# A two-layer decode kernel: heads in twos, one on even and one on odd partitions, loaded in runs of 24576 B

## The chip, the core and the metric

The kernel runs on one core of a Trainium2 chip (trn2). The metric is device time in microseconds (us) of one launch; lower is better. Each kernel is run several times and the median counts. One execution is profiled: its trace tells, for each engine, when each instruction ran, and for the 16 DMA engines when each packet moved.

Names used below: PE is TensorE (matmuls; PEld its weight loads), DVE is VectorE, ACT is ScalarE, POOL is GpSimd, SP is the engine whose queue issues all DMAs here. L12 is line 12 of the kernel.

## What is computed

One token (B = S = 1, D = 640) goes twice through attention against a cache and then a small mixer with an MLP; both layers use the same weights and the same caches. Of 32768 cached positions the last W = 4096 are used, by 32 heads of width 192. All inputs are bf16.

```python
def attention(x, k_cache, v_cache, wq, wo):          # x: LayerNorm of the token
    q = (x @ wq) as 32 heads of 192
    k, v = k_cache[:, :, Sk - 4096:], v_cache[:, :, Sk - 4096:]
    p = softmax(q . k * 192 ** -0.5)                 # per head, over 4096 positions
    return concat over heads (p . v) @ wo
def mixer_mlp(x, w1, w2, w3, w4):
    ...
    return x1 + gelu(layernorm(x1) @ w3) @ w4
for _ in range(2):
    x = x + attention(layernorm(x), k_cache, v_cache, wq, wo)
    x = x + mixer_mlp(layernorm(x), w1, w2, w3, w4)
```

With S = 1 the shifted `w1`, `w2` branch of the mixer brings zeros, so `x1` is the mixer's input and only `w3` and `w4` are loaded. K and V of a layer are 32 heads x 2 x 1.57 MB, 100 MB; the work is small beside these bytes.

## The kernel before

**Cells.** SBUF holds 11 cells, each 128 partitions x 12288 B, as much as K or V of one head. `take` gives the cell that has been free longest, `give` puts it back. A cell holds K, V, a block of Wo (four heads), W3, W4, a transposed K that is kept for the second layer (`("T", h)`), or the area in which transposed quarters of K lie (`("area", layer)`, one cell, its four quarters in turn).

**The stream.** `layer_stream` writes out the order of all transfers of a layer by hand; `need(...)` issues them on SP in that order, as far as the one asked for. Per group of four heads it is K of the next group's head, V of this group's head, four times, and then Wo of the group. SP works in order: a transfer whose cell is not free yet holds up all that are behind it. Eight semaphores for DMAs are used in turn, so the ninth transfer also waits for the first one to land. Wq is loaded first; W3 and W4 close each layer.

**One head of K (L360 to L380, L443 to L456).** K of a head is loaded with 32 positions on each of the 128 partitions: one run of 12288 B a partition. `T` turns it on DVE in 32x32 blocks, a quarter at a time (L377, four a head). `scores`, called as `S`, multiplies it on PE with a block-diagonal Q (`Qblk`, 16 columns for the group's four heads by four parts; L453, 24 matmuls of 128x256 a head) and all four heads of a group add up in one half of the PSUM tile `ST_ps`.

**Softmax of a group (L473 to L540).** `part_max` and `full_max` reduce on DVE (L478, L488), PE turns and spreads the maxima (L483, L501), ACT forms Exp (L507), DVE turns P (L512), PE swaps it into place (L523) and ACT writes `PT` (L526).

**P.V (L560 to L576).** 16 matmuls a head (L569) with two columns of `PT` each write `O_ps`; DVE transposes `O_ps` for each head (L576), and `o_fold` brings the head's part into `oT` with small matmuls (L583, L588). The cell of V is given back behind the 16 matmuls.

**The order around it.** For each group: scores of the next group's first head while the softmax of this group runs; then for each head of this group its P.V, and T and S of the next group's next head.

**From layer to layer.** Groups go from heads 28 to 31 down to heads 0 to 3 in the first layer and upward in the second. Transposed K of heads 0 to 6 stays in cells (`NKEEP` = 7), V of head 3 (`VC`) too, V of head 2 (`VP`) is kept in PSUM and in the cell of Wo's block 0, a part of V of head 4 (`VX`) in `kx`. So the second layer starts with scores of heads 0 to 3 from kept cells, and with loads of V of heads 0 and 1, K of head 7, then K of head 8, V of head 4, and so on. In the first group of the second layer the P.V go in the order 3, 0, 1, 2. Cells that the loads there use: V of head 0 the cell of W3 (free after L901), V of head 1 the cell of W4 (free after L948), K of heads 7 and 8 the cells of T0 and T2 (free after the scores of heads 0 and 2, L453), V of heads 4 and 5 those of T3 and T6.

Of the kernel before, what the change touches and what calls it, by code (L numbers as in the profile page):

```python
# [35 lines left out]
def kernel(  # L36
# [33 lines left out]
    scale = float(Dh) ** -0.5  # L70
    eps = 1e-5
# [39 lines left out]

    loaded = {}
    free = deque(range(NCELL))
    cell_of = {}

    def take(key):
        i = free.popleft()
        cell_of[key] = i
        return cells.tile([P, FREE], BF16, tag=f"cell{i}", name=f"cell{i}")
# [9 lines left out]

    def load_k(layer, h):  # L130
        t = take(("k", layer, h))
        nc.sync.dma_start(t[:], A_k_cache[0, h, s0:Sk, :].rearrange("(p j) d -> p (j d)", p=P))
        return t

    def load_v(layer, h):
        t = take(("v", layer, h))
        src = A_v_cache[0, h, s0:Sk, :].rearrange("(p j) d -> p (j d)", p=P)
# [4 lines left out]
        for e in cut + (FREE,):  # L142
            kept_v = h == VP or h == VX and i > 0
            if layer == 0 or not kept_v:
                nc.sync.dma_start(v_pair(t, h, i, e - i), src[:, i:e])
            i = e
# [58 lines left out]
    def layer_stream(layer):  # L205
# [38 lines left out]
        return seq  # L244
# [4 lines left out]
    def need(*key):  # L249
        while key not in loaded:  # L250
            k = stream[pos[0]]
            pos[0] += 1
            loaded[k] = LOADERS[k[0]](*k[1:])
        return loaded[key]
# [9 lines left out]
    ones = const.tile([P, P], F32, name="ones")  # L264
    nc.vector.memset(ones[:], 1.0)
    Lf = wx_sb[:, 0:2 * P].bitcast(F32).rearrange("p (j i) -> p j i", j=4)
    nc.gpsimd.memset(Lf, 0.0)
    for base in (0, -1, -64, -65):
# [29 lines left out]
    nc.vector.tensor_reduce(out=hm[:], in_=ident[:].rearrange("p (q x m) -> p x q m", q=4, m=NM)[:, 0:QH],  # L298
                            op=ALU.add, axis=AX.XY)

    QW = QH * NM
    QHEAD = NCOL * QW
    QSLOT = QH * (QHEAD + NM)
# [18 lines left out]
    def ln_center(x, rowsum):  # L322

        mean_ps = psm.tile([P, 1], F32, tag="psm")
        nc.tensor.matmul(mean_ps[:], lhsT=ones[:], rhs=rowsum[:, 0:1], start=True, stop=True)
# [10 lines left out]
        def total():  # L336
            var_ps = psm.tile([P, 1], F32, tag="psm")
            nc.tensor.matmul(var_ps[:], lhsT=ones[:], rhs=ssq[:, 0:1], start=True, stop=True)
# [43 lines left out]
    def qproj_steps(c, xc, part=None, row=None):  # L382
# [49 lines left out]
        def block():  # L432
            nh = n * P // Dh
            h0 = 4 * (t0 - c * QT) // NCOL
            diag = Qblk[:, c % 2].rearrange("p (h r) -> p h r", h=QH)[:, h0:h0 + nh, 0:QHEAD]
            nc.vector.tensor_tensor(
                out=diag.rearrange("p h (f x) -> p h f x", x=QW)[:, :, :, 0:NM],
                in0=held["r"][:, :].rearrange("p (h f) -> p h f", h=nh).unsqueeze(3).broadcast_to([P, nh, NCOL, NM]),
                in1=blkm[:, :].unsqueeze(1).unsqueeze(1).broadcast_to([P, nh, NCOL, NM]), op=ALU.mult)
# [3 lines left out]
    def scores(h, Ts, q0, ST_ps, hq):  # L443

        ng = NGK // NT
        Q = Qblk[:, h // QH % 2, hq * QHEAD:(hq + 1) * QHEAD].rearrange("p (f x) -> p f x", x=QW)
# [26 lines left out]
    def softmax_steps(n, ST_ps, sc):  # L473
        held = {}

        def part_max():
            pm = big.tile([P, 1], F32, name="pm")
            nc.vector.tensor_reduce(out=pm[:], in_=ST_ps, op=ALU.max, axis=AX.X)  # L478
            held["pm"] = pm

        def turn_max():
            pmT_ps = psm.tile([1, P], F32, tag="psm")
            nc.tensor.transpose(pmT_ps[0:1, :], held["pm"][:, 0:1], ident[:, :])  # L483
            held["pmT"] = pmT_ps

        def full_max():
            ngm = big.tile([1, 2 * QH], F32, name="ngm")
            nc.vector.tensor_reduce(out=ngm[:], in_=held["pmT"][0:1, :].rearrange("o (q x m) -> o x q m", q=4, m=NM),  # L488
                                    op=ALU.max, axis=AX.XY, negate=True)
            held["PrT"] = o_bytes[:, SW:2 * SW]  # L490

            wide = held["PrT"][0:1, :].bitcast(F32)
            nc.vector.tensor_scalar(
                out=wide.rearrange("o (q x m) -> o q x m", q=4, m=NM),
                in0=ngm[:].unsqueeze(1).unsqueeze(3).broadcast_to([1, 4, 2 * QH, NM]),
                scalar1=sc[0:1, 0:1], scalar2=None, op0=ALU.mult)
            held["w"] = wide

        def spread_max():
            nb_ps = psm.tile([P, 1], F32, tag="psm")  # L500
            nc.tensor.matmul(nb_ps[:], lhsT=held["w"],  # L501
                             rhs=ones[0:1, 0:1], start=True, stop=True)
            nb_sb = big.tile([P, 1], F32, name="nb_sb")
            nc.scalar.copy(nb_sb[:], nb_ps[:])  # L504
            Pr = o_bytes[:, 0:SW]
            lpart = big.tile([P, 1], F32, name="lpart")
            nc.scalar.activation(out=Pr, in_=ST_ps, func=ACTF.Exp,  # L507
                                 bias=nb_sb[:, 0:1], scale=sc[:, 0:1], accum_out=lpart[:, 0:1])
            held["Pr"], held["l"] = Pr, lpart

        def turn_p():
            nc.vector.transpose(held["PrT"], held["Pr"])  # L512
            lh = big.tile([P, QH], F32, name="lh")
            nc.vector.tensor_scalar(out=lh[:], in0=hm[:], scalar1=held["l"][:, 0:1], scalar2=None, op0=ALU.mult)
            held["lh"] = lh

        def swap():
            ng = NGK // NT
            PT_ps = psm.tile([P, n, NJ4, NGK], F32, tag="psm")
# [5 lines left out]
            PT = big.tile([P, n, NJ4 * NGK], BF16, name="PT")  # L525
            nc.scalar.copy(PT[:].rearrange("p h c -> p (h c)"), PT_ps[:].rearrange("p h j g -> p (h j g)"))  # L526
            l_ps = psm.tile([P, QH], F32, tag="psm")
            nc.tensor.matmul(l_ps[:], lhsT=ones[:], rhs=held["lh"][:], start=True, stop=True)  # L528
# [31 lines left out]
    def pv(layer, h, hq, PT, mid=None):  # L560
# [4 lines left out]
        for i in range(NB):  # L565
# [3 lines left out]
            nc.tensor.matmul(O_ps[r:r + 2, :], lhsT=PT[:, hq, 2 * i:2 * i + 2],  # L569
# [433 lines left out]
```

## Time and profile before

Three runs: 519.72, 520.05 and 520.63 us; the median is 520.05. The profiled execution took 519.73 us; its span, from the first to the last instruction, is 517.8 us.

| busy | us | share of the span | instructions |
|---|---|---|---|
| PE | 321.8 | 62% | 4084 |
| PEld | 190.0 | 37% | 4084 |
| DVE | 294.9 | 57% | 591 |
| ACT | 48.9 | 9% | 173 |
| POOL | 4.0 | 1% | 16 |
| DMA queue of SP, mean of 16 engines | | 99.0% | 24052 packets, 216.48 MB |

The costliest groups are L377 (DVE transposes of K, 228 of 944 ns), L453 (scores, 1536 matmuls, recorded at 383 ns each, many at once), L569 (P.V) and L576 (DVE transposes of `O_ps`, 64 of 580 ns). The mean rate of the DMA engines is 419 GB/s over the span and 424 to 433 GB/s in most slices.

How to read it: in a row of slices each digit is the busy share of one fortieth of the span in tenths. A row of windows gives a stretch in us, then busy us (and instructions) of PE, PEld, DVE, ACT and POOL, the granted PE clock, the DMA engines' share and GB/s. In a timeline each line is start, duration, engine, source line, operation. The chain of waits follows the work back from its end; each line is start, duration and what the time went to. Two packets of one DMA engine can overlap by a few ns in the records, so a share of DMA can read 1.01.

### The profile page before, as it was taken

The numbers are of one execution on the slowest core, as the hardware profiler recorded it, in microseconds if no ns is written. First come the engines' busy times: TensorE is split into PE (matmuls) and PEld (weight loads), VectorE is DVE, ScalarE is ACT, GpSimd is POOL, SyncE is SP. The second block draws the span as 40 slices with busy tenths as digits, with TensorE's granted clock in tenths as the row PEclk, the third lists the DMA queues.
The fourth block names the chain that finished last, engine by engine and source line by source line (L and its number), as shares of the span: only waits on it lengthen the run. The fifth ranks groups of instructions, "written<-read, shape, count | busy, mean of one in ns | idle before, by whom it ended". The sixth has DMA issues, their size and how long they took to land.

```text
span 517.8 us, 9464 instructions
## 1 busy us (share of the span) xinstructions
PE 321.8 (62%) x4084; PEld 190.0 (37%) x4084; DVE 294.9 (57%) x591; ACT 48.9 (9%) x173; POOL 4.0 (1%) x16
## 2 busy tenths in 40 slices
PE   1057656666655655767755866668666667648665
PEld 0024333333332433434333634334333334425334
DVE  2067767575584764666624264756576766664722
ACT  1000101010010100001011001001010101001011
POOL 2000000000000000000000000000000000000000
PEclk9997778565585776677665567657787865776855
DMA  8999999999999999999999999999999999999996
GB/s 348 432 429 426 429 428 429 429 429 424 433 426 427 432 425 428 429 427 428 426 420 401 377 424 430 428 424 427 433 428 427 429 429 427 426 432 427 427 417 250
DMA packets 24093, 217.08 MB, mean 419 GB/s; under 512 B 2548, under 2 KB 3060, under 8 KB 8692
## 3 DMA queue, kind: packets, MB, share of 16 engines
q1 hardware_dynamic: 24052, 216.48, 99.0%
q8 instruction: 32, 0.52, 0.4%
q14 instruction: 9, 0.07, 0.0%
HBM read 216.47 MB, written 0.00 MB: 418 GB/s over the span
## 4 chain that ended last, share of the span: by engine, by line
DMA 50%; PE 23%; DVE 22%; issue 3%; ACT 1%; SPq 1%; DVEq 0%; ACTq 0%
DMA cell<-in_A_k_cache_dram 28%; DVE cell L377 16%; DMA cell<-in_A_v_cache_dram 16%; PE ST_ps L453 10%; PE O_ps L569 7%; DMA cell<-in_A_wo_dram 4%; DVE o_sb L576 2%; DMA cell<-in_B_w_dram 2%; DVE pm L478 1%; PE nb_ps L501 1%; DVE o_sb L512 1%; ACT o_sb L507 1%; PE l_ps L528 1%; PE PT_ps L523 1%; PE qT_ps L407 1%
## 5 line engine op out<-in xcount | busy, mean ns | idle before, releaser
L453 PE MATMUL ST_ps<-cell,Qblk 128*16 128x256 bf16 x1536 | 163.8, 383 | 108.2 <-DVE cell L377 70.1
L377 DVE STREAM_TRANSPOSE cell<-cell 128x768 uint32<-128x768 uint32 x228 | 204.0, 944 | 14.6 <-DMA cell<-in_A_k_cache_dram 14.3
L453 PEld LDWEIGHTS <-Qblk 128*16 128x16 bf16 x1536 | 85.8, 112 | 178.2 <-issue 151.0
L569 PE MATMUL O_ps<-cell,PT 128*2 128x384 bf16 x1018 | 98.7, 456 | 7.5 <-DMA cell<-in_A_v_cache_dram 5.5
L576 DVE STREAM_TRANSPOSE o_sb<-O_ps 128x384 f32<-128x384 f32 x64 | 37.1, 580 | 109.5 <-PE O_ps L569 109.4
L569 PEld LDWEIGHTS <-PT 128*2 128x2 bf16 x1024 | 45.6, 100 | 21.2 <-issue 11.4
L512 DVE STREAM_TRANSPOSE o_sb<-o_sb 128x256 bf16<-128x256 bf16 x16 | 7.1, 445 | 33.4 <-ACT o_sb L507 22.5
L584 ACT ACTIVATE oT<-oT_ps,rl 32x6 bf16<-32x6 f32 x40 | 10.3, 257 | 162.9 <-PE oT_ps L583 156.7
L583 PE MATMUL oT_ps<-o_sb,Lq 128*32 128x6 f32 x160 | 13.8, 195 | 10.4 <-DVE o_sb L576 9.9
L583 PEld LDWEIGHTS oT_ps<-o_sb,Lq 128*32 128x32 f32 x160 | 13.1, 145 | 19.4 <-issue 15.6
L589 ACT ACTIVATE oT<-oT_ps,rl 32x6 bf16<-32x6 f32 x24 | 6.2, 257 | 107.1 <-PE ST_ps L453 86.8
L407 PE MATMUL qT_ps<-xc,wq_sb 128*128 128x1 bf16 x210 | 7.2, 165 | 13.1 <-DMA wq_sb<-in_A_wq_dram 12.2
L523 PE MATMUL PT_ps<-o_sb,Eq 128*32 128x32 bf16 x256 | 7.2, 237 | 9.2 <-DVE o_sb L512 4.1
L421 DVE TENSOR_TENSOR Xq<-qT_ps,maskq 128x24 bf16<-128x24 f32 (+1 forms) x18 | 2.9, 159 | 17.4 <-PE qT_ps L407 17.4
L523 PEld LDWEIGHTS <-Eq 128*32 128x32 bf16 x256 | 5.4, 109 | 19.3 <-issue 19.2
L407 PEld LDWEIGHTS <-wq_sb 128*128 128x128 bf16 x210 | 6.8, 103 | 14.3 <-DMA wq_sb<-in_A_wq_dram 13.3
L504 ACT COPY nb_sb<-nb_ps 128x1 f32<-128x1 f32 x16 | 2.5, 159 | 96.2 <-PE nb_ps L501 96.2
L396 PE MATMUL qr_ps<-wq_sb,xc 128*1 128x384 bf16 x90 | 11.5, 398 | 0.0
L615 PE MATMUL yr_ps<-cell,oT 128*1 128x320 bf16 x108 | 10.8, 346 | 0.0
L528 PE MATMUL l_ps<-lh,ones 128*128 128x4 f32 x32 | 7.5, 306 | 4.9 <-ACT PT L526 4.9
L588 PE MATMUL oT_ps<-o,Lq 128*32 128x6 f32 x48 | 6.0, 198 | 6.5 <-DVE o L587 6.5
L428 PE MATMUL Qrep_ps<-Xq,Lb 128*128 128x24 bf16 (+1 forms) x18 | 3.2, 178 | 10.7 <-DVE Xq L421 10.4
(145 smaller groups left out, 196.7 us busy)
## 6 DMA issues: line engine op xcount, KB each, us to landing
cell<-in_A_k_cache_dram SPq DMA_DIRECT2D x57, 1536.0 KB, 25.2
cell<-in_A_v_cache_dram SPq DMA_DIRECT2D x56, 1536.0 KB, 25.3
cell<-in_A_wo_dram SPq DMA_DIRECT2D x13, 960.0 KB, 25.7
wq_sb<-in_A_wq_dram SPq DMA_DIRECT2D x5, 1536.0 KB, 12.5
cell<-in_A_v_cache_dram SPq DMA_DIRECT2D x6, 768.0 KB, 22.9
cell<-in_A_v_cache_dram SPq DMA_DIRECT2D x2, 1248.0 KB, 9.8
cell<-in_B_w_dram SPq DMA_DIRECT2D x1, 1536.0 KB
cell<-in_B_w_dram SPq DMA_DIRECT2D x2, 768.0 KB, 10.3
```

The lines of the kernel that those rows point to most:

```text
L377: nc.vector.transpose(Tu, Ku[:, :, q * NY:(q + 1) * NY])
L396: nc.tensor.matmul(qr_ps[32 * i:32 * i + 1, :], lhsT=xc[:, kc:kc + 1], rhs=wq_sb[:, kc, t0 * P + i * N:t0 * P + (i + 1) * N], start=(kc == ...
L407: nc.tensor.matmul(qT_ps[:, tl:tl + 1], lhsT=wq_sb[:, kc, t * P:(t + 1) * P], rhs=xc[:, kc:kc + 1], start=(kc == 0), stop=(kc == ND - 1))
L453: nc.tensor.matmul(ST_ps[r:r + QW, :].rearrange("p (g i) -> p g i", g=ng), lhsT=Q[:, n, :], rhs=T4[:, :, f, :, t], start=(hq == 0 and n == ...
L512: nc.vector.transpose(held["PrT"], held["Pr"])
L523: nc.tensor.matmul(PT_ps[32 * m:32 * (m + 1), :, :, ng * q:ng * (q + 1)], lhsT=Eq[:, q, :], rhs=src[:, m:QW:NM], start=True, stop=True)
L528: nc.tensor.matmul(l_ps[:], lhsT=ones[:], rhs=held["lh"][:], start=True, stop=True)
L569: nc.tensor.matmul(O_ps[r:r + 2, :], lhsT=PT[:, hq, 2 * i:2 * i + 2], rhs=v_pair(V, h, 2 * i * Dh, 2 * Dh), start=(i < 4), stop=(i >= NB - 4))
L576: nc.vector.transpose(o_sb[:], O_ps.rearrange("p (e a c) -> p e c a", e=2, c=NA))
L583: nc.tensor.matmul(oT_ps[r, :], lhsT=Lq[:], rhs=o_sb[:, e, :, e], start=(e == 0), stop=(e == 1))
L584: nc.scalar.activation(oT[r, :], oT_ps[r, :], ACTF.Copy, scale=rl[r, 0:1])
L615: nc.tensor.matmul(yr_ps[32 * i:32 * i + 1, :], lhsT=oT[:, k:k + 1], rhs=wo_t[:, k * D + i * N:k * D + (i + 1) * N], start=(k == 0), stop= ...
```

## The change

Heads are loaded, scored and multiplied with V in twos, h and h + 1 with h even. Their 2 x 4096 positions lie on 128 partitions so that head h is on the even ones and head h + 1 on the odd ones, 64 positions on each: 24576 B that follow each other in HBM. A pair fills two cells side by side (`cells_sb` is now one tile), the first cell with the first 32 positions of each partition, the second with the other 32. Each cell so holds half of both heads.

- **Loads.** K of heads from 8 on, and V of heads 8 to 31 in the first layer and 6 to 29 in the second, go as one transfer a pair (`load_both`), at the place of the even head in the stream; the odd head's place falls away. The others are loaded a cell at a time in runs of 12288 B (`half_heads`).
- **Cells.** `take_pair` looks for two free neighbours, the first even, and takes those that have been free longest. `take`, for a single cell, prefers a free cell whose neighbour is not free, as long as a pair stands among the next four transfers.
- **Scores.** `Qblk` has 32 columns for each matmul in place of 16 (16 for each head of the pair); the count of matmuls and their 256 columns stay.
- **Softmax.** Even and odd columns of `ST_ps` belong to even and odd heads, so maximum, bias and Exp are made for each: two transposes, two reductions, two small matmuls, two Exp over 128 columns in place of one over 256; rows of the other heads get a bias of -1e30. `swap` moves 64 columns in place of 32.
- **P.V.** Four columns of `PT` in place of two; both heads of a pair add up in `O_ps`, and DVE transposes it once a pair; `o_fold` works for two heads.
- **Order.** In the first group of the second layer P.V goes 3, 2, 0, 1.
- `ones` becomes a broadcast of one column.

```diff
+    cells_sb = cells.tile([P, NCELL * FREE], BF16, name="cells")
+    free = list(range(NCELL))
     def take(key):
-        i = free.popleft()
+        lone = [i for i in free if i ^ 1 not in free] if pairs_ahead() else []
+        i = (lone or free)[0]
+        free.remove(i)
         cell_of[key] = i
-        return cells.tile([P, FREE], BF16, tag=f"cell{i}", name=f"cell{i}")
+        return cell(i)
+
+    def take_pair(*keys):
+        ends = [(max(free.index(i), free.index(i + 1)), i) for i in free if i % 2 == 0 and i + 1 in free]
+        if not ends:
+            return None
+        i = min(ends)[1]
...
+    def two_heads(cache, h):
+        return cache[0, h:h + 2, s0:Sk, :].rearrange("e (p j) d -> p e (j d)", p=P // 2)
+
+    def half_heads(cache, h):
+        return two_heads(cache, h // 2 * 2)[:, :, h % 2 * FREE:(h % 2 + 1) * FREE]
+
+    def load_both(kind, cache, layer, h):
+        keys = [(kind, layer, h + n) for n in range(2)]
+        i = take_pair(*keys)
+        if i is None:
+            return {key: LOADERS[kind](*key[1:]) for key in keys}
+        nc.sync.dma_start(cell(i, 2), two_heads(cache, h))
+        return {key: cell(i + n) for n, key in enumerate(keys)}
...
-        return seq
+        return [(k[0] + "2",) + k[1:] if both(*k) else k for k in seq if not (both(*k) and k[2] % 2)]
+
+    def both(kind, layer, h=0):
+        return kind == "k" and h >= 8 or kind == "v" and 8 - 2 * layer <= h < H - 2 * layer
+
+    def pairs_ahead():
+        return any(k[0] in ("k2", "v2") for k in stream[pos[0]:pos[0] + 4])
...
         def full_max():
...
+            for e in range(2):
+                rows = wide[:, e * P:(e + 1) * P].rearrange("o (q e x) -> o q e x", q=NT, e=2)
+                nc.vector.memset(rows[:, :, 1 - e], NEVER)
+                nc.vector.tensor_reduce(
+                    out=ngm[0:1, e], in_=own[:, e].rearrange("o (q x) -> o q x", q=NT)[:, :, 0:HB].rearrange(
+                        "o q (r z) -> o r q z", r=2), op=ALU.max, axis=AX.XY, negate=True)
+                nc.vector.tensor_scalar(
+                    out=rows[:, :, e].rearrange("o q (r z) -> o q r z", r=2),
+                    in0=ngm[0:1, e].unsqueeze(1).unsqueeze(3).broadcast_to([1, NT, 2, 2 * NM]),
+                    scalar1=sc[0:1, 0:1], scalar2=None, op0=ALU.mult)
...
+            for e in range(2):
+                nc.scalar.activation(out=by_head(Pr)[:, e], in_=by_head(ST_ps)[:, e], func=ACTF.Exp,
+                                     bias=nb_sb[:, e:e + 1], scale=sc[:, 0:1], accum_out=lpart[:, e:e + 1])
...
-            nc.tensor.matmul(O_ps[r:r + 2, :], lhsT=PT[:, hq, 2 * i:2 * i + 2],
-                             rhs=v_pair(V, h, 2 * i * Dh, 2 * Dh), start=(i < 4), stop=(i >= NB - 4))
+            nc.tensor.matmul(O_ps[r:r + 4, :], lhsT=PT[:, hq, 2 * i:2 * i + 2].rearrange("p c e -> p (c e)"),
+                             rhs=v_pair(V, h, 2 * i * Dh, 2 * Dh), start=(first and i < 4),
+                             stop=(not first and i >= NB - 4))
...
-        nc.vector.transpose(o_sb[:], O_ps.rearrange("p (e a c) -> p e c a", e=2, c=NA))
+        if not first:
+            nc.vector.transpose(o_sb[:], O_ps.rearrange("p (e a c) -> p e c a", e=2, c=NA))
...
             if layer == 1 and gi == 0:
-                order.insert(0, order.pop(cur.index(VC)))
-            for hq, h in order:
-                pv(layer, h, hq, PT, fold)
+                order = [order[n] for n in (VC, VP, 0, 1)]
+            for n, (hq, h) in enumerate(order):
+                first = n % 2 == 0
+                pv(layer, h, hq, PT, first, fold)
```

## The prediction

> **What bounds the kernel now.** I read the page's share of the DMA engines first, then the windows by stage, then SP's timeline and the chain of waits where the windows show a hole.
>
> The page, its span, its slices and its queue:
>
> ```profile
> span 517.8 us, 9464 instructions
> DMA  8999999999999999999999999999999999999996
> q1 hardware_dynamic: 24052, 216.48, 99.0%
> cell<-in_A_k_cache_dram SPq DMA_DIRECT2D x57, 1536.0 KB, 25.2
> ```
>
> The 16 DMA engines are full for the whole span, and a K transfer lands 25.2 us (median) after its issue though its own data takes 3.65 us: about seven transfers queue. So time falls if the bytes flow faster, and rises by whatever the engines stand idle; the margin of a transfer's issue is how long the queue lasts. It isn't the same everywhere. Windows: stretch, length, busy us (instructions) of PE, PEld, DVE, ACT, POOL, clock, DMA share, GB/s:
>
> ```profile
> 100.00:230.00 130.00, 81.21 (x929) 47.25 (x932) 78.17 (x138) 11.23 (x38) 0.00 (x0) 0.64 1.01 428
> 283.00:291.00 8.00, 5.24 (x134) 4.19 (x131) 2.56 (x19) 1.46 (x7) 0.00 (x0) 0.50 0.93 339
> 291.00:320.00 29.00, 20.29 (x348) 12.52 (x346) 13.85 (x30) 2.57 (x10) 0.00 (x0) 0.68 1.01 422
> ```
>
> Between the layers the share falls to 0.93 against 1.01 (packets overlap a little): some 0.6 us idle. SP's own timeline there, then the chain (start, us, what):
>
> ```profile
> 283.12 0.33 SPq L145 DMA_DIRECT2D cell<-in_A_v_cache_dram  x1
> 287.24 0.33 SPq L145 DMA_DIRECT2D cell<-in_A_v_cache_dram  x1
> ...
> 291.10 3.75 SPq L132 DMA_DIRECT2D cell<-in_A_k_cache_dram  x2
> 296.80 0.33 SPq L145 DMA_DIRECT2D cell<-in_A_v_cache_dram  x1
> 299.69 0.33 SPq L132 DMA_DIRECT2D cell<-in_A_k_cache_dram  x1
> 300.37 0.33 SPq L145 DMA_DIRECT2D cell<-in_A_v_cache_dram  x1
> ```
>
> ```profile
> 285.35 1.88 PE y_ps L948 x60
> ...
> 289.59 1.46 PE ST_ps L453 x24
> 291.05 0.13 PE Qrep_ps L428
> 291.18 1.39 PE ST_ps L453 x22
> ...
> 310.64 1.44 PE ST_ps L453 x11
> ...
> 315.91 0.70 PE O_ps L569 x12
> ```
>
> Here SP issues one transfer at a time, each the moment a cell comes free, and the queue is empty: V of head 1 goes out at 287.24, when the last matmul on W4 (L948) frees its cell, and the packet records have v0's last packets at about 289.0 and v1's first at 289.4, 2.1 us after the issue. Any later issue here is idle DMA, and since the queue is full from 291 to the end (share 1.00 to 1.01), the end moves by as much.
>
> **The change, part by part.**
>
> *Longer runs.* The built program has 48 paired transfers (24 of K, 24 of V), so none falls back to single loads. Packet records: on one engine packets of 12288 B start 456.5 ns apart, of 7680 B 287.0 ns, and the 4 B one that ends a transfer 5.9 ns before the next. The line through the first two is 0.03677 ns a byte plus 4.7 ns a packet. Each pair sends 128 packets less, 8 on each engine, and one ending packet less: 8 x 4.7 + 5.9 = 43.5 ns, x48 = **-2.1 us**. Bounds: 0 if a run of 24576 B is cut in two again; -3.5 if the recorded durations (460 ns for 12288 B, 291 for 7680 B: 7.3 to 7.9 ns a packet) hold, 48 x (8 x 7.9 + 9). I take the spacing, since the queue moves by it. Rows of two heads alternate 12 MiB apart in HBM; the nearest row is the 96 KiB between the runs that the engines read now, at 428 GB/s, so I price it at nothing, and 1% of the 151 MB paired (353 us at 428 GB/s), 3.5 us, as the far end.
>
> The Trainium skill, DMA: Bandwidth & Descriptors, "Why small descriptors are slow (HBM only)", gives about 3 fixed cycles a packet; at its 850 MHz that is 3.5 ns, and this part would be an estimated -1.4 us where the records' 4.7 ns make -1.8. The same page, "Latency and other measured facts", speaks against the change: rows at a pitch of 4 or 8 MiB ran at half rate. 12 MiB is such a multiple, and halving the paired bytes would add an estimated 353 us; no run here shows it, and only pairs of rows lie so.
>
> *Steady groups.* A group brings K pair, V pair, K pair, V pair and Wo, 4 x 7.27 + 2.3 = 31.4 us, and each pair slot is refilled one group later. A K slot is free when its eight transposes are done (8 x 0.86 us, part of them behind the softmax, some 10 us after landing), a V slot after its PV (some 8 us); the refill isn't due until 24 us after landing. So 14 us of margin covers the doubled grain: **0**. Without that cover each late microsecond would cost itself.
>
> *Softmax, folds.* Per group DVE loses two O_ps transposes (2 x 0.58 us) and gains a reduce (0.27), a tensor_scalar (0.27), two memsets and an add (0.15 each); PE and ACT gain a transpose, a 1x1 matmul pair (0.29) and half an Exp with its read (0.4): about 1.8 us later in the chain to P, hidden behind the queue in the groups above: **0**. S and PV keep count and columns: 0.
>
> *Wait A: v1's cell.* In layer 1 SP issues v0, v1, k7, (k8,k9), v4, v5, (k10,k11), (v6,v7), Wo. `take` now prefers a free cell whose partner isn't free. When v1 asks, W4's cell 1 and the cells of T0 to T3 (7, 3, 6, 0) are on the list; only 3 is lone (2 holds head 3's V). So v1, which had W4's cell, gets T1's, and in the built program it waits for the last score matmul of head 1 in layer 1: 291.18 + 1.39 = 292.57 by the chain, not 287.24. k7, given W4's free cell, stands behind it on SP. First packet 292.57 + 2.1 = 294.7, v0's data ends at 289.0: 5.7 us idle against 0.6 now: **+5.1 us**. Bounds 4.3 (Q of layer 1 a little sooner) to 5.6 (slower issue of a two-level address).
>
> *Wait B: v5's cell.* From 294.7: v1 3.65, k7 3.65, (k8,k9) 7.27 (its cells, T2's and T0's, are free at 294.5), v4 2.98 (T5's, free by 300.4): dry at 312.2. v5 goes by the same rule to lone cell 3, v1's own, and waits for the last PV matmul of v1, which is last of group 0 (order 3, 2, 0, 1). Before, it had T6's cell at 300.37. When is that PV done? Before, head 7's scores end at 312.1 and three PVs with an O_ps transpose between each follow to 316.6. After: the softmax is 1.8 us later, but T(7) no longer waits for an O_ps transpose (0.58 us) nor the issue behind it (0.72): scores about 0.2 us later; then PV 2, a transpose, PV 0 and PV 1 with none between, 0.7 us less: about 315.9 (315.2 to 317.5). First packet 318.0: 5.8 us idle, **+5.8 us** (4.9 to 7.4). (k10,k11), whose cells are free since 300, (v6,v7) and Wo are queued behind v5; with them issued the queue holds some 17 us, and the waits behind are covered again.
>
> *End of layer 0.* Single loads, as before, with issues as little as 3.6 us ahead (Wo at 254.21); cells are others, but each is released by the same work: 0, far end +3.6 (1.8 us in each of two groups).
>
> *Sum*, on the profiled execution's 519.73 (span 517.8 and 1.9 around it): 519.73 - 2.1 + 5.1 + 5.8 = 528.5. The runs' median is 520.05, 0.3 higher: **528.8 us**, 1.7% slower.
>
> **Rivals.** *The waits hide (faster).* If the queue still held data at 287 and 312, only the longer runs would count: 520.05 - 2.1 = 517.9. It needs 5 us of margin at v1, where the trace shows the engines already idle for 0.6. It decides below 1 us of idle in both. For it: everywhere else the margin is 10 us or more. *Only A (slower, less).* If group 0's PVs end by 310, B is filled: 520.05 - 2.1 + 5.1 = 523.1. Against it: head 7's scores alone end at 312. *More goes wrong (slower still).* No gain from the runs, or 1% lost by the two-head rows: 528.8 + 2.1 = 530.9, up to 534.4; or the end of layer 0 runs dry: 532.4. For it: margins of 3.6 us; against: the releases are the same.
>
> **How the numbers follow.** The forecast 0.62, only A 0.10, more goes wrong 0.21, the waits hide 0.07. A measurement here tells 0.2% (1 us) from no change. Bounds of the forecast itself: 520.05 - 3.5 + 4.3 + 4.9 = 525.8 and 520.05 - 0 + 5.6 + 7.4 = 533.1. The range takes in only A's time at its lower end: 523 to 533. Faster 0.06, within 0.2% 0.02, slower 0.92.
>
> **What would show it.** In the new trace: packets of 24576 B some 908 ns apart (else the first term is wrong); two holes in the DMA slices, near 288 to 293 and 311 to 317; SP's V issue held until scores of head 1 and the next one until a PV ends; no hole elsewhere, and about 431 GB/s in steady groups. If the holes are missing, or are filled by the end, the prediction falls.

## The result, and the profile after

The changed kernel takes 528.95 us (median of 6 runs, 526.8 to 531.05) where the kernel before takes 519.88 us (6 runs): the ratio is 1.0170, with a 95% interval of 1.0144 to 1.0196. The profiled execution took 527.9 us, its span is 525.8 us, 8.0 us more than before. In what follows v1 is V of head 1, k7 is K of head 7, and (k8,k9) is one paired transfer. A hole is a stretch in which the DMA engines stand idle; the margin of an issue is the time from it to the end of the data that is queued ahead of it. The page of the changed kernel, lines of the span, the DMA slices and the queue:

```profile
span 525.8 us, 9517 instructions
DMA  8999999999999999999999689999999999999995
GB/s 343 442 428 431 419 442 428 429 437 431 427 435 429 427 427 427 429 390 427 429 382 401 237 378 388 433 432 421 442 432 426 434 431 423 441 431 426 434 407 237
q1 hardware_dynamic: 17140, 216.48, 97.5%
```

And the rates of the kernel before, in its own 40 slices:

```profile
GB/s 348 432 429 426 429 428 429 429 429 424 433 426 427 432 425 428 429 427 428 426 420 401 377 424 430 428 424 427 433 428 427 429 429 427 426 432 427 427 417 250
```

Between its ends the DMA row held nothing but nines; now it has a 6 and an 8 next to each other, slices 23 and 24 of 13.1 us each, 289 to 316 us. In bytes the dent is wider than in busy time: 237, 378 and 388 GB/s, and already 390 in slice 18 and 382 in slice 21 (427 and 420 before), where the DMA row still shows 9. So there is a second loss, in which the engines count as busy and yet move less. The windows of the changed kernel (stretch, length, busy us of PE, PEld, DVE, ACT and POOL, granted clock, DMA share, GB/s) show the same:

```profile
100.00:230.00 130.00, 79.49 (x937) 47.51 (x934) 75.63 (x151) 11.13 (x38) 0.00 (x0) 0.67 1.00 427
225.00:240.00 15.00, 10.78 (x171) 7.43 (x167) 11.27 (x22) 1.70 (x8) 0.00 (x0) 0.83 1.00 393
258.00:283.00 25.00, 13.91 (x200) 7.91 (x199) 7.27 (x28) 2.67 (x11) 0.00 (x0) 0.56 1.00 399
283.00:291.00 8.00, 5.29 (x161) 4.84 (x162) 3.07 (x25) 1.96 (x9) 0.00 (x0) 0.50 0.95 358
291.00:320.00 29.00, 21.84 (x387) 14.11 (x379) 15.16 (x42) 2.57 (x10) 0.00 (x0) 0.79 0.79 309
330.00:430.00 100.00, 58.57 (x710) 33.65 (x702) 58.14 (x115) 8.90 (x30) 0.00 (x0) 0.67 1.00 430
```

The rows of the kernel before that the prediction does not show:

```profile
225.00:240.00 15.00, 9.21 (x121) 5.75 (x120) 9.82 (x16) 1.54 (x6) 0.00 (x0) 0.77 1.01 429
258.00:283.00 25.00, 14.62 (x240) 9.10 (x238) 8.26 (x30) 3.42 (x14) 0.00 (x0) 0.57 1.01 417
330.00:430.00 100.00, 66.53 (x804) 37.62 (x796) 64.98 (x113) 9.90 (x33) 0.06 (x1) 0.70 1.01 428
```

From 291 to 320 the share is 0.79 (1.01 before): 6 us of 29. From 330 on it is back at 1.00 with 430 GB/s (428 before). SP's timeline in the changed kernel (start, us, what; a line with x2 runs from the first issue's start to the second one's end):

```profile
284.29 10.06 SPq L177 DMA_DIRECT2D cells<-in_A_v_cache_dram  x2
294.44 1.35 SPq L164 DMA_DIRECT2D cells<-in_A_k_cache_dram  x1
295.89 0.58 SPq L159 DMA_DIRECT2D cells<-in_A_k_cache_dram  x1
299.09 15.83 SPq L177 DMA_DIRECT2D cells<-in_A_v_cache_dram  x2
314.97 0.60 SPq L159 DMA_DIRECT2D cells<-in_A_k_cache_dram  x1
315.66 0.56 SPq L159 DMA_DIRECT2D cells<-in_A_v_cache_dram  x1
```

v0 goes out at 284.29, and its line ends at 294.35 with v1, which was held until 293.81; k7 and (k8,k9) come right behind. v4 goes out at 299.09, and its line ends at 314.92 with v5, held until 314.38; (k10,k11) and (v6,v7) come right behind. The DMA row of a close window, 288 to 298 us in 40 slices of 0.25 us, then the one of 311 to 321 us:

```profile
DMA  9594949453320000000000003000982796959899
```

```profile
DMA  3994994994943211009950849959393959969799
```

Some 5 us of nothing behind the first wait, hardly 1.5 us behind the second. The 9s and 5s that follow each hole are packets that take longer than their size needs: 12288 B usually take 460 ns, and here up to 1358 ns behind the first hole and 1527 behind the second.

To compare the kernels, I added up from the packet records, for each stretch, the idle time of the mean engine and the "stretched" time (what packets took beyond the usual of their size, over 16 engines). In us, idle + stretched:

```
                 225-240      258-283      283-291      291-320      320-340
before         0.00+0.03    0.03+0.11    0.82+0.85    0.07+0.44    0.00+0.07
changed        0.17+1.04    0.06+1.13    0.59+0.55    6.25+1.91    0.02+0.07
e1_neither     0.18+1.03    0.18+1.34    0.40+0.54    1.57+1.93    0.00+0.07
e2_only_a      0.17+1.20    0.05+1.04    0.85+0.37    4.08+0.85    2.85+0.61
e3_only_b      0.08+0.97    0.05+1.17    0.60+0.53    5.36+2.12    0.23+0.67
e4_split       0.03+0.43    0.08+1.16    0.23+0.41    5.96+2.46    0.08+0.33
e5_before_a    0.00+0.03    0.00+0.10    2.20+0.29    2.63+0.62    0.00+0.03
e6_half_rows   0.00+0.03    0.02+0.78    0.95+0.55    0.43+0.49    0.00+0.07
e7_k_first     0.00+0.09    0.11+1.23    0.79+0.51    1.69+1.68    0.00+0.06
e8_all         0.00+0.08    0.22+1.08    0.35+0.60    0.35+0.81    0.81+0.52
e9_k12_alone   0.00+0.09    0.15+1.25    0.62+0.61    0.58+0.55    0.00+0.07
e10_k12_split  0.00+0.06    0.12+1.23    0.34+0.37    0.83+0.90    0.00+0.03
e11_old_rows   0.00+0.09    0.09+0.31    0.67+0.53    0.19+0.36    0.00+0.07
e12_all_again  0.00+0.08    0.19+0.94    0.33+0.54    0.44+0.78    0.64+0.88
```

Changed less before: 1.2 us at 225 to 240, 1.05 us at 258 to 283, 7.1 us at 283 to 320. The experiments take these three apart, and the gain of the longer runs besides.

### The profile page after: what moved, and what is told of

It reads as the page before. It is cut to its first block, busy times and chain, and to the rows that moved or that the text cites. A ratio compares the mean times of both kernels' runs of the same rounds, so it can differ in the third digit from the quotient of the medians.

```text
span 525.8 us, 9517 instructions
## 1 busy us (share of the span) xinstructions
PE 315.3 (60%) x4132; PEld 194.8 (37%) x4132; DVE 285.0 (54%) x642; ACT 48.6 (9%) x173; POOL 4.0 (1%) x16
## 4 chain that ended last, share of the span: by engine, by line
DMA 54%; DVE 21%; PE 18%; ACT 3%; issue 2%; SPq 1%; ACTq 0%; DVEq 0%
DMA cells<-in_A_k_cache_dram 43%; DVE cells L423 15%; PE ST_ps L502 8%; DMA cells<-in_A_v_cache_dram 7%; DMA cells<-in_B_w_dram 4%; PE O_ps L630 3%; ACT o_sb L566 2%; PE nb_ps L558 2%; DVE o_sb L571 1%; PE PT_ps L583 1%; PE pmT_ps L536 1%; PE y_ps L701 1%; DVE pm L530 1%; PE y_ps L1012 1%; DVE wx_sb L689 1%
## 5 line engine op out<-in xcount | busy, mean ns | idle before, releaser
L423 DVE STREAM_TRANSPOSE cells<-cells 128x768 uint32<-128x768 uint32 x228 | 203.7, 945 | 53.1 <-DMA cells<-in_A_k_cache_dram 52.5
L502 PE MATMUL ST_ps<-cells,Qblk 128*32 128x256 bf16 x1536 | 147.9, 367 | 121.1 <-DVE pm L530 67.1
L502 PEld LDWEIGHTS <-Qblk 128*32 128x32 bf16 x1536 | 89.6, 121 | 177.2 <-issue 158.0
L630 PE MATMUL O_ps<-cells,PT 128*4 128x384 bf16 x1018 | 93.5, 450 | 7.5 <-DMA cells<-in_A_v_cache_dram 7.0
L639 DVE STREAM_TRANSPOSE o_sb<-O_ps 128x384 f32<-128x384 f32 x32 | 18.6, 583 | 80.6 <-PE O_ps L630 80.6
L630 PEld LDWEIGHTS <-PT 128*4 128x4 bf16 x1024 | 41.7, 102 | 25.9 <-issue 18.0
L566 ACT ACTIVATE o_sb<-ST_ps,nb_sb,sc 128x128 bf16<-128x128 f32 x32 | 14.9, 489 | 0.5
L558 PEld LDWEIGHTS nb_ps<-one,o_sb 1*128 1x128 f32 x64 | 12.2, 261 | 7.3 <-issue 5.0
L558 PE MATMUL nb_ps<-one,o_sb 1*128 1x1 f32 x64 | 13.7, 309 | 1.6 <-DVE ngm L546 1.1
L679 PE MATMUL yr_ps<-cells,oT 128*1 128x320 bf16 x108 | 13.7, 413 | 0.0
```

The costliest lines, as they stand in the source:

```text
L423: nc.vector.transpose(Tu, Ku[:, :, q * NY:(q + 1) * NY])
L502: nc.tensor.matmul(ST_ps[r:r + QW, :].rearrange("p (g i) -> p g i", g=ng), lhsT=Q[:, n, :], rhs=T4[:, :, f, :, t], start=(hq == 0 and n == ...
L558: nc.tensor.matmul(nb_ps[:, e:e + 1], lhsT=held["w"][:, e * P:(e + 1) * P], rhs=one[0:1, 0:1], start=True, stop=True)
L566: nc.scalar.activation(out=by_head(Pr)[:, e], in_=by_head(ST_ps)[:, e], func=ACTF.Exp, bias=nb_sb[:, e:e + 1], scale=sc[:, 0:1], accum_out ...
L630: nc.tensor.matmul(O_ps[r:r + 4, :], lhsT=PT[:, hq, 2 * i:2 * i + 2].rearrange("p c e -> p (c e)"), rhs=v_pair(V, h, 2 * i * Dh, 2 * Dh), ...
L639: nc.vector.transpose(o_sb[:], O_ps.rearrange("p (e a c) -> p e c a", e=2, c=NA))
```

## The experiments

The kernel before ran beside each series, at 519.2 to 519.4 us; where kernels of different series are compared, it is by the ratio to it.

**The two waits, one by one.** Wait A is that of v1 for its cell, wait B that of v5. Cells are given out by a list, so one line can force them:

```diff
+    WANT = {("v", 1, 1): 1, ("k", 1, 7): 3}
...
-        i = (lone or free)[0]
+        i = WANT.get(key, (lone or free)[0])
```

This is e1_neither. e2_only_a has `{("v", 1, 5): 1}`, e3_only_b both entries of e1 and `("v", 1, 5): 1`, which there is v1's cell.

> Layer 1: v1 gets W4's cell again and k7 takes T1's, so SP no longer holds v1 until the scores of head 1; v5's cell (3) is then k7's, free long before. Theory (the two holes are the loss): the 5.1 us idle near 291 to 295 and the 1.4 us near 314 to 316 go, some 0.6 us idle stays at 289 as in the kernel before, and the stretched packets after the holes go too (up to 1.2 us): 528.9 - 5.1 - 1.4 + 0.6 = 523.0, down to 521.8. The 2 us that the end of layer 0 lost stay. Rival (the end is set by the later softmax and PV chain, the holes are only where it shows): 527 or more, with idle DMA elsewhere after 291.

> Only wait A is left: v5 takes k7's cell (1) instead of v1's, and (v6,v7) the cells of k8 and k9. Theory (A is the price, B only what A leaves): hole near 291 to 295 as in the changed kernel, none at 314: 528.9 - 1.4 = 527.5 (to 526.5 with the slow packets behind it). Rival (B costs the 5.8 us that were predicted for it, and the trace of one execution shows too little): 523.

> Only wait B is left: v1 gets W4's cell, k7 T1's, and v5 waits for the last PV of v1, in whose cell it goes. Theory (the holes do not add; PVs of group 0 are set by the scores, not by the loads, so without A the queue runs dry 5 us sooner and B grows to 5 to 6 us): hole only near 309 to 315, total 528.9 - 5.1 - 1.4 + 5.5 + 0.6 = 528.5 (526.5 to 529). Rival (the holes add, B stays at 1.4): 528.9 - 5.1 + 0.6 = 524.4.

Measured: e1_neither 523.71 us (ratio 1.0081, 1.0067 to 1.0095), e2_only_a 528.35 (1.0173, 1.0159 to 1.0186), e3_only_b 527.52 (1.0152, 1.0138 to 1.0166). The stretch from 291 to 320 us in the windows, first e1_neither, then e3_only_b:

```profile
291.00:320.00 29.00, 21.99 (x389) 14.48 (x389) 15.21 (x42) 2.58 (x10) 0.00 (x0) 0.79 0.96 380
```

```profile
291.00:320.00 29.00, 22.01 (x381) 14.47 (x374) 15.17 (x42) 2.58 (x10) 0.00 (x0) 0.79 0.83 322
```

So the waits are the loss in this place: without both the share rises from 0.79 to 0.96, and PE and DVE work as long as in the changed kernel; the rival that the compute chain sets the end falls. But the holes do not add. Taking A away alone gains hardly anything (1.0152 against 1.0170, intervals that overlap), since B's hole then opens from 1.4 to 4.1 us, 309 to 315; SP of e3_only_b:

```profile
298.08 15.67 SPq L178 DMA_DIRECT2D cells<-in_A_v_cache_dram  x2
313.80 0.60 SPq L160 DMA_DIRECT2D cells<-in_A_k_cache_dram  x1
```

v5 goes out at 313.22 (the line's end less 0.53), only 1.2 us sooner than in the changed kernel, while the queue runs dry 5 us sooner, from 309 on: the last PV of v1 hangs on scores and softmax, not on the loads. e2_only_a does not answer what B costs. It gave (v6,v7) the cells of k8 and k9, and these are free late; SP of e2_only_a, and its window from 320 to 330:

```profile
309.38 0.56 SPq L160 DMA_DIRECT2D cells<-in_A_k_cache_dram  x1
326.11 0.54 SPq L160 DMA_DIRECT2D cells<-in_A_v_cache_dram  x1
```

```profile
320.00:330.00 10.00, 7.21 (x135) 5.29 (x138) 4.87 (x14) 1.59 (x6) 0.71 (x2) 0.50 0.72 284
```

B's hole is gone and a new one stands at 324 to 327 (2.85 us idle): the wait was moved, not removed. e1_neither in turn came out 0.7 us above my estimate (1.1 by the ratio). One cause is that k7 now waits for T1's cell: it goes out at 293.95, and 0.75 us of idle follow between 294 and 297.5. SP of e1_neither:

```profile
284.45 4.65 SPq L178 DMA_DIRECT2D cells<-in_A_v_cache_dram  x2
293.95 0.54 SPq L165 DMA_DIRECT2D cells<-in_A_k_cache_dram  x1
295.16 0.83 SPq L160 DMA_DIRECT2D cells<-in_A_k_cache_dram  x1
298.81 10.81 SPq L178 DMA_DIRECT2D cells<-in_A_v_cache_dram  x2
```

**Wait A in the kernel before.** The same force on cells, with `{("v", 1, 1): 4, ("k", 1, 7): 9, ("v", 1, 2): 3}`; 4 is T1's cell there, 9 W4's.

> The kernel before, with wait A alone put into it: in layer 1 v1 takes T1's cell and k7 W4's, so v1 is held until the scores of head 1; runs stay 12288 B, heads go one by one. Theory (the place of the cell is enough, the paired loads and the longer softmax have no part in it): v1 is issued near 292.6 instead of 287.2, some 5 us idle there, nothing after it: 519.4 + 4.0 to 5.1 = 523.4 to 524.5. Rival (the queue of single loads refills soon enough, and A hurts only with pairs behind it): 521 or less.

Measured: 523.37 us (ratio 1.0080, 1.0066 to 1.0094), +4.1 us. SP of this kernel, and its window:

```profile
282.91 9.77 SPq L148 DMA_DIRECT2D cell<-in_A_v_cache_dram  x2
292.77 1.20 SPq L135 DMA_DIRECT2D cell<-in_A_k_cache_dram  x2
```

```profile
283.00:291.00 8.00, 5.34 (x130) 4.19 (x131) 2.60 (x20) 1.46 (x7) 0.00 (x0) 0.50 0.72 282
```

The place of one cell is enough; neither paired loads nor the softmax is needed for it. Behind this hole, from 295.5 to 320 us, nothing runs dry (0.00 us idle): SP has its singles out in time.

**The longer runs.** In e4_split the changed kernel loads each pair by two transfers into the same cells; e10_k12_split does this to e9_k12_alone (below), which has hardly a hole left.

```diff
-        nc.sync.dma_start(cell(i, 2), two_heads(cache, h))
+        for n in range(2):
+            nc.sync.dma_start(cell(i + n), half_heads(cache, h + n))
```

> Same cells, same waits, but each pair is loaded by two transfers in runs of 12288 B, one for each cell. Theory (24576 B runs save 8 x 4.7 + 5.9 ns for each of 48 pairs): +2.1 us, 531.0, packets 456.5 ns apart again. Rival 1 (the longer runs bring nothing): 528.9. Rival 2 (two-head rows 12 MiB apart cost up to 1%): faster than the changed kernel only if the pattern was the cost, which these loads keep in halves: 527 or less.

> As e9_k12_alone, every remaining pair loaded by two transfers in runs of 12288 B, in the same cells and order. Theory (with hardly a hole left, the whole of the longer runs' gain shows: 47 pairs x 43.5 ns): e9_k12_alone + 2.0, 520.0. Rival (the gain is only 1 us, as e4_split seemed to say): e9_k12_alone + 1.

Measured: e4_split 529.81 us (ratio 1.0205, 1.0192 to 1.0219), against 1.0170 of the changed kernel 0.35%, 1.8 us. e10_k12_split 522.78 us (522.56 to 523.0) against 519.77 (518.9 to 520.41): 3.0 us; in the two profiled executions the last packets end 2.3 us apart. The runs do what was said of them: packets of 24576 B start 908 ns apart (median), twice 456.5 less 5. That they bring nothing falls by e10, whose interval (1.0056 to 1.0083) lies clear of e9's (1.0000 to 1.0017); e4's still touches that of the changed kernel, and e4 loses 0.6 us less than it in the stretches of the table. But neither run changes the length of the runs alone: the split loads also read halves of runs, rows of two heads in turn, a pattern that costs time elsewhere (below). The spacing gives 2.0 us for 47 pairs; of the other 1.0 us in e10, 0.6 is stretched time in the first 40 us, where the queue is just filling.

**The end of layer 0.** Two theories for its 2.2 us. In the changed kernel k5's load stands behind both heads of (v8,v9); before, it stood behind v8 alone. DVE's timeline of the changed kernel shows what waits for it:

```profile
210.87 1.84 DVE L423 STREAM_TRANSPOSE cells<-cells 128x768 uint32<-128x768 uint32 x2 [2.51 <-DMA cells<-in_A_k_cache_dram]
```

Before, these transposes start at 207.82. All that follows is late, by 3 us at first, down to v4's cell, and SP issues v4 at 226.53 instead of 222.25. First the kernel before, then the changed one:

```profile
207.82 1.83 DVE L377 STREAM_TRANSPOSE cell<-cell 128x768 uint32<-128x768 uint32 x2
222.25 0.33 SPq L145 DMA_DIRECT2D cell<-in_A_v_cache_dram  x1
```

```profile
226.53 0.53 SPq L177 DMA_DIRECT2D cells<-in_A_v_cache_dram  x1
```

The 16 engines do not reach v4 at the same time. Told apart by which packet follows on which, the last one ends the data ahead of v4 4.5 us after the issue (9.4 before; I took 4.8 and 9.7), the first one 0.8 us after it (6.0 before). The other theory: the single loads are not as before. They take half of each 24576 B run, 64 rows of one head and 64 of another in turn. e6_half_rows puts that pattern into the kernel before; e7_k_first is e1_neither with the order changed alone, in the same cells:

```diff
+    def rows(cache, h):
+        if h >= 8:
+            return cache[0, h, s0:Sk, :].rearrange("(p j) d -> p (j d)", p=P)
+        two = cache[0, h // 2 * 2:h // 2 * 2 + 2, s0:Sk, :].rearrange("e (p j) d -> p e (j d)", p=P // 2)
+        return two[:, :, h % 2 * FREE:(h % 2 + 1) * FREE]
```

```diff
+    AHEAD = [[(("k", 0, 5), ("v2", 0, 8)), (("k", 0, 7), ("v2", 0, 10))], []]
...
+        for a, b in AHEAD[layer]:
+            out.remove(a)
+            out.insert(out.index(b), a)
```

> The kernel before, but K and V of heads 0 to 7 are read in the pattern of the changed kernel's single loads (half of each 24576 B run, 64 rows of each of two heads), so that these heads are computed from other rows than the reference's; times of everything else are untouched. Theory (the 1.4 us of stretched packets at the end of layer 0 come from a queue that is nearly dry there): 519.4, stretched packets as in the kernel before. Rival (the pattern itself is slower to read): 520.8, with stretched packets of 9984, 2304 and 4608 B between 225 and 283 us.

> As e1_neither (523.7), and in layer 0 k5 is issued ahead of (v8,v9) and k7 ahead of (v10,v11), in the same cells. Theory (a pair carries the head that is not due yet ahead of the K that is: k5 lands 3.65 us later, the work of the last groups of layer 0 is 3 us late, the margin of v4's issue falls from 9.7 to 4.8 us and packets stretch): k5 lands near 207.2 instead of 210.9, v4's issue is some 3 us earlier, the 1.0 us of stretched packets at 225 to 240 go: 522.5 (521.5 to 522.9). Rival (the pattern of the half-row loads stretches them whatever the margin): 523.7.

Measured: e6_half_rows 521.24 us (ratio 1.0038, 1.0025 to 1.0050), e7_k_first 521.55 (1.0047, 1.0034 to 1.0059), by the ratios 1.8 us under e1_neither, of which 1.1 us are idle and stretched time at 225 to 240. e6's own theory, no loss, fell; its rival was right about 258 to 283 and wrong about 225 to 240, where the same pattern stretches nothing (0.03). So both theories hold, each in its own place. Windows from 225 to 240 us, changed kernel above in the result, here e7_k_first:

```profile
225.00:240.00 15.00, 10.34 (x140) 6.39 (x139) 7.95 (x18) 1.41 (x6) 0.00 (x0) 0.61 1.02 429
```

and SP of e7_k_first, with v4 at 223.10:

```profile
223.10 0.54 SPq L178 DMA_DIRECT2D cells<-in_A_v_cache_dram  x1
223.69 0.60 SPq L178 DMA_DIRECT2D kx<-in_A_v_cache_dram  x1
```

393 GB/s became 429 with the same pattern and 3.4 us more margin (4.2 us on the first engine in place of 0.8): here it was the order. From 258 to 283, where v2's two pieces go out late in any kernel (264.55 before, 265.73 in the changed one), the order changes nothing (1.34 us stretched in e1_neither, 1.23 in e7_k_first), and the kernel before gets two thirds of the changed one's loss by the pattern alone (0.11 to 0.78). The pattern costs 2.0 us in e6's runs, more than these 0.7 us; 0.4 us more are lost at 291 to 320, and the last packet of its profile ends 1.7 us later than before. The rest I can't place.

**All of it mended, and what is left.** e8_all is e7_k_first with k7 in T0's cell (two more entries keep the other cells in place) and (k10,k11) ahead of v5:

```diff
+    WANT = {..., ("T", 0): 3, ("T", 1): 7, ("v", 0, 4): 9, ("k", 0, 1): 0}
+    AHEAD = [[...], [(("k2", 1, 10), ("v", 1, 5))]]
```

e9_k12_alone is e8_all with k12 and k13 of layer 1 loaded alone, each as its own cell comes free (`AHEAD` puts k12 ahead of wo1, k13 ahead of (v8,v9)):

```diff
+        if (kind, layer, h // 2) == ("k", 1, 6):
+            return False
```

e11_old_rows is e8_all with its single loads in the old pattern; e12_all_again is e8_all unchanged, beside e11.

```diff
+    def rows(cache, h):
+        return cache[0, h, s0:Sk, :].rearrange("(p j) d -> p (j d)", p=P)
...
-        nc.sync.dma_start(t, half_heads(A_k_cache, h))
+        nc.sync.dma_start(t, rows(A_k_cache, h))
...
-        src = half_heads(A_v_cache, h)
+        src = rows(A_v_cache, h)
```

> As e7_k_first, and T0 and T1 change cells in layer 0, so that k7 of layer 1 takes T0's cell, free after the scores of head 0, and not T1's; and (k10,k11) is issued ahead of v5, whose cell is free only 9 us later. Theory (the thin stretch of e1_neither between 290 and 312, some 2 us of idle and 1.2 us of stretched packets more than before, comes from k7 held until 293.95 and v5 until 309.08): 522.5 - 2.0 = 520.5 (519.5 to 521.5). Rival (the later start of layer 1's chain holds everything, whichever cell k7 has): 522 to 523. With all losses gone the longer runs would leave 517.3.

> As e8_all (519.2), with k12 and k13 of layer 1 loaded alone into the same two cells, k12 issued ahead of wo1, in the cell of k8, k13 ahead of (v8,v9). Theory (the hole of e8_all at 328 to 330, 0.8 us idle and 0.5 us of stretched packets, is the pair's grain: (k12,k13) waits for both k8's and k9's cell, and k8's is free at 310): 519.2 - 1.2 + 0.05 = 518.0 (517.6 to 518.4), below the kernel before. Rival (the next issue, of (v8,v9) or (k14,k15), runs dry in its place): 519.2.

> As e8_all, but the single loads of K and V (heads 0 to 7, 30 and 31) read 128 rows of 12288 B of one head in a row, as the kernel before does, so that these heads are computed from other rows than the reference's. Theory (what keeps e8_all from the 517.1 that the longer runs leave is the half-row pattern of its single loads, 2.0 us by e6_half_rows): 517.2 (516.7 to 517.8), and the stretched packets of 7680 and 4608 B at 258 to 283 us gone. Rival (the pattern costs only what stretched packets show, 0.6 us): 518.6. Rival 2 (margin alone): 519.2.

> e8_all once more, beside e11_old_rows on the same chip; its profiled execution was 1.2 us above its own median, and this one is to tell whether the hole at 328 to 330 us belongs to the kernel. Theory (it does not, which is why e9_k12_alone did not gain): 519.2 and no hole there. Rival (it does, in most executions): 519.2 with a hole of 0.5 us or more at 325 to 331.

Measured: e8_all 519.20 us, and 519.67 as e12_all_again (ratio 1.0005 both times, 0.9996 to 1.0014); e9_k12_alone 519.77 (1.0009, 1.0000 to 1.0017); e11_old_rows 517.98 (0.9983, 0.9967 to 0.9999). So the two waits, the order and k7's cell (with the place of (k10,k11)) account for 1.65 of the 1.70 per cent lost; but the 2 us that the longer runs bring do not appear, so as much is still lost elsewhere. e8 did better than its theory (519.5 to 521.5 us), e11 a little worse than its own (516.7 to 517.8). e11_old_rows computes some heads from other rows, so no kernel here that does the whole task beats the one before by what can be measured. Windows of e8_all, then of e11_old_rows:

```profile
258.00:283.00 25.00, 14.21 (x236) 8.82 (x236) 7.57 (x33) 3.27 (x14) 0.00 (x0) 0.55 1.01 399
291.00:320.00 29.00, 22.35 (x348) 14.12 (x337) 13.81 (x35) 2.58 (x10) 0.00 (x0) 0.62 1.00 417
320.00:330.00 10.00, 7.07 (x119) 4.62 (x119) 6.20 (x21) 1.60 (x6) 0.05 (x1) 0.67 0.95 389
330.00:430.00 100.00, 64.94 (x825) 39.66 (x822) 63.27 (x121) 9.31 (x31) 0.66 (x2) 0.72 1.00 429
```

```profile
258.00:283.00 25.00, 14.42 (x236) 9.10 (x236) 7.99 (x39) 3.74 (x15) 0.00 (x0) 0.52 1.01 412
291.00:320.00 29.00, 21.70 (x410) 14.79 (x403) 15.53 (x44) 3.73 (x15) 0.00 (x0) 0.78 1.01 426
320.00:330.00 10.00, 5.61 (x76) 3.32 (x76) 6.34 (x15) 0.45 (x1) 0.71 (x2) 0.66 0.99 422
330.00:430.00 100.00, 61.59 (x784) 37.29 (x784) 61.23 (x119) 9.56 (x32) 0.00 (x0) 0.74 1.01 432
```

e8_all still moves 399 GB/s from 258 to 283, where the old pattern moves 412, and has a new thin place at 328, where (k12,k13) waits for k8's and k9's cell together. That hole is there in both profiles (0.81 and 0.64 us idle between 320 and 340), so e12's theory fell. Yet e9, whose profile has no such hole, is no faster: against e8's, its profile loses some 0.4 us between 258 and 291 and 0.5 us after 480. Why stays open. It is not shown either that the pair made the hole, because the granted PE clock differs too; e8_all, then e9_k12_alone, then e11_old_rows:

```profile
291.00:300.00 9.00, 8.70 (x169) 5.86 (x162) 2.94 (x8) 0.46 (x2) 0.00 (x0) 0.50 0.98 385
291.00:300.00 9.00, 7.56 (x180) 5.26 (x179) 4.19 (x15) 0.47 (x2) 0.00 (x0) 0.87 0.96 385
291.00:300.00 9.00, 7.51 (x179) 5.58 (x172) 4.22 (x15) 0.62 (x3) 0.00 (x0) 0.88 1.00 416
```

In e8 and e12 the clock stays at 0.50 here, and the 72 score matmuls before the softmax take 4.03 us; in e9 and e11 it is 0.87 and 0.88, and in e11 they take 2.25. With the old pattern (k12,k13) goes out at 323.78 instead of 328.25 and no hole arises; 0.9 us of that is the earlier start of layer 1's scores, some 2.4 us the clock. Whether the pattern has a part in the clock, no run shows. In the runs 0.9 us (by the ratio) to 1.2 us (by the medians) of the longer runs' gain remain.

## Why the prediction was right

It gave 528.8 us and two holes in their places, for these reasons; but the size of wait B and the nothing for the end of layer 0 were wrong, in opposite directions.

*Longer runs, -2.1 us: right.* 908 ns and 431 GB/s were expected, 908 ns and 430 GB/s are there, 1.8 to 3.0 us in the two comparisons. Of the two rules of the Trainium skill weighed against this step, both from DMA: Bandwidth & Descriptors: the one on row pitch ("Latency and other measured facts"), by which rows 4 or 8 MiB apart are copied at half rate, does not show in rows that alternate 12 MiB apart; and the fixed cost of a packet is better taken as the records' 4.7 ns than as the 3 cycles of "Why small descriptors are slow (HBM only)", estimated at 3.5 ns, since one packet of 24576 B takes 5 ns less than two of 12288 B (908 against 913, from start to start). The times of e4 and e10 cannot tell 1.4 us from 1.8.

*Wait A, +5.1 us: right.* v1 was held for the scores of head 1, until 293.81 (292.57 expected; the scores of layer 1 began 1.2 us late, behind a layer 0 that ended late, as said below). The hole is 5.1 us of idle where 5.7 were expected; less the 0.65 that stood there before, that is +4.4, inside the bounds of 4.3 to 5.6. The same wait in the kernel before costs 4.1 us.

*Wait B, +5.8 us: the mechanism right, the size wrong.* v5 did wait for v1's last PV, but for 1.4 us of idle. "Dry at 312.2" was really 314.0: after A the stream began later and ran thin for 3 us (1.9 us of stretched packets between 291 and 320), all of which my sum put at full rate. And "about 315.9" was 314.35, though layer 1's scores began 1.2 us later than before. By its own terms the sum even gives 316.4: 1.8 less 0.58 and 0.72 is 0.5, not 0.2, and 316.6 + 0.5 - 0.7 is 316.4. T(7) does follow PV 3 directly, 1.3 us sooner than before, as reckoned. Two terms were off. I added 1.8 us of softmax, the trace has 1.0 us (first step of the maximum to PT's copy: 5.2 us against 4.2). And I left the granted clock where it was: from 291 to 300 us it was 0.78 in place of 0.55, so that the score matmuls took less. The last 72 of them, before and after:

```profile
297.24 3.08 PE L453 MATMUL ST_ps<-cell,Qblk 128*16 128x256 bf16 x72 [0.35 <-DVE Qblk L436]
297.49 2.25 PE L502 MATMUL ST_ps<-cells,Qblk 128*32 128x256 bf16 x72 [0.30 <-DVE Qblk L484]
```

With them the maximum starts at 299.78 instead of 300.38, which made B's hole smaller; nothing in the prediction foresaw it. The step that failed is the addition itself: a hole upstream delays the running dry downstream, while the release there is set by compute. Without A, B's hole is 4.1 us where I had computed 5.8 (e3_only_b). A and B together, by e1_neither, are 0.9%, 4.6 us, where the sum had 10.9; with k7's wait, which takes their place, and what stays stretched, the stretch from 283 to 320 loses 7.1 us.

*End of layer 0, 0: wrong, +2.2 us.* The prediction put nothing here; "Single loads, as before" is the step that failed, twice over. They aren't as before (half-row pattern), and the pairs put a head that isn't due ahead of a K that is. I had looked at which work releases each cell, and it is the same; I had not followed when that work can start. The far end, 3.6 us, held it.

*Steady groups and softmax, 0: right.* From 330 to 430 us nothing is idle and the margins of the paired issues are 8.6 us or more (I had 14).

So 10.9 us for the waits was 3.8 us too much, and the end of layer 0 was 2.2 us too little; that the total came out within 0.2 us is partly luck. Put together, -2.1, 7.1 and 2.2 are 7.2 us of the 8.0 by which the two profiled spans differ; the medians differ by 9.1, and the 1.9 us between stay open. Of the rivals, "only A" came closest in kind: B's hole was nearly filled, but by A's own delay.

## What to carry to other kernels

In a stream that one queue issues in order, price a hole by when the queue runs dry and when the release comes, both after all holes upstream, and the release also by the clock that the matmuls before it may be granted: two waits of 5 us may cost 5 together, and removing one may gain nothing. Where loads are made coarser, list what each coarse load is now ahead of, not only what it waits for; a buffer of two neighbouring cells is free when the later one is. And look at bytes per second beside the busy share: while packets are stretched the engines count as busy (393 GB/s at a share of 1.00, from 225 to 240 us).

## What the runs showed of the hardware

A nearly dry queue shows as stretched packets, not only as idle time. Here it took a short margin and the new pattern together: v4's load was stretched with the new pattern and 0.8 us of margin on the first engine (0.92 of the 1.04 us at 225 to 240), not with the new pattern and 4.2 or more (0.09 in e7_k_first, 0.03 in e6_half_rows); and the late v2 cost 0.11 us with the old pattern, 0.78 with the new one. From the packet records, v1's load into a dry queue: in e5_before_a (128 rows of one head) it is issued at 292.35, the engines' first packets start 1.0 to 1.8 us later, most of them take 0.9 to 1.3 us, and from the second on each takes 460 ns. In the changed kernel (half runs, rows of two heads in turn) it is issued at 293.81, the first packets start 1.3 to 2.7 us later, and up to six of an engine's first packets take more than 470 ns, the longest 1358. The Trainium skill, DMA: Bandwidth & Descriptors ("Latency and other measured facts"), gives some 600 ns to the first byte of a transfer issued from such a queue. The traces come near it for the first engine, if it is counted from the end of SP's issue (0.65 us in e5_before_a, 0.78 in the changed kernel); the last engine starts 1.45 and 2.1 us after that end. SP also takes longer to issue it: 0.54 us for the new patterns, 0.33 us for the old one. With margin enough the half-row pattern costs nothing: the singles between 240 and 258 us move at 456 ns a packet (median) in both kernels. What in the pattern makes it slow to start was not tried.
